# The 512 outputs of a decode step as eight rows of 64 on partitions 16 apart, by products in four column groups

## The chip, the cores and the metric

The kernel runs on one core of a Trainium2 chip. Its engines are TensorE (PE; its loading of weights is shown as PEld), VectorE (DVE), ScalarE (ACT), GpSimd (POOL) and SyncE (SP), which here only issues transfers; 16 DMA engines move the data. The metric is the device time of one execution in microseconds (us), the median of the runs. The kernel before takes 354.38 us (3 runs, 354.29 to 354.51).

## The reference, cut to what matters

One token of width 512 passes a block with modulated layer norms (shift, scale and gate from a vector c), an attention over a cache of 32768 positions with 32 query heads on 8 key/value heads, and a feed-forward part of 512 by 1792 by 512.

```python
mod = (_silu(c) @ w_mod).reshape(c.shape[0], 6, 1, -1)
sa, ca, ga, sb, cb, gb = (mod[:, 0].copy(), mod[:, 1].copy(), mod[:, 2].copy(), mod[:, 3].copy(), mod[:, 4].copy(), mod[:, 5].copy())
h = _layernorm(x, axis=-1) * (1 + ca) + sa
x = x + ga * _A_ref(h, A_k_cache, A_v_cache, A_wq, A_wo)
h = _layernorm(x, axis=-1) * (1 + cb) + sb
x = x + gb * _B_ref(h, B_w1, B_w2)
return x
```

`_A_ref` is the attention with its projections wq and wo, `_B_ref` is `relu(h @ w1) @ w2`. The change touches the last line of it: how `h @ w2`, the gate gb and the residual x are laid out when they meet.

## The kernel before, in words

All large tensors come by one queue, SP's, in an order written out by hand (`stream`): half of the first keys, w_mod, wq, then keys and values of the eight groups, then wo in four pieces, w1 in one, and w2 in five pieces (`W2P`: slices 0 to 4, 5 to 9, 10 and 11, 12, 13; a slice is 128 rows of w2, one row in each partition). They land in a ring of three slots; the last slot, `tail_sb`, holds wo, w1, w2 and some small work areas.

At the front, POOL and DVE make constants out of an identity matrix while the first transfers run: `cmask` (which group of 16, 8 or 4 partitions a partition belongs to), `place32` (a partition's number modulo 32, one column for each), and `rowpick`, of 34 columns, of which 30 to 33 hold a one where the partition belongs to that quarter of 32. The vectors c and x are brought into columns (L248, L254), the six modulation vectors are computed from w_mod (L324) and turned into columns `modT_sb`.

The middle is a loop over eight groups of heads. For each, DVE transposes the keys (L441), PE computes scores (L460), softmax runs on ACT and DVE, and PE multiplies with the values (L523). `build_qbd` (L415, on POOL) makes the weights of the scores for each group and reads the four ones of `rowpick` as a mask. PE's and DVE's order is written out by hand (`manual_schedule`).

The end: `project` multiplies with wo; x1T, the residual after attention, stands as 128 partitions by 4 columns. `layernorm_T` follows, and while its sums run (`meanwhile`), `expand` and `four_rows` turn x1T into four rows of 128 on partitions 30 to 33: DVE multiplies the columns with `place32` into 128 by 128 (L356), and one product with `rowpick` as weights sums them into the rows (L365). The gate `gb` takes the same way much earlier (L372). Then come 16 products with w1 (L765), a transpose and the relu (L775, L776) into `hid_st`, a strip of zeros with one hidden column every 32, and the products with w2 (L788): four for each slice, of 128 columns each. Output column block i belongs on partition 30 + i; the window of 32 (or 2) columns of `hid_st` that serves as weights is chosen so that the hidden column falls on that row, and the other rows get zeros. So blocks 0 and 1 go to the first column group of the array (partitions 0 to 31), and 2 and 3 to the second. At last DVE multiplies with the gate rows (L793), adds the residual rows (L795), and SP stores four rows of 256 bytes (L796). `keep_clock` issues products whose result is not used, between the steps of the tail.

Of the kernel before, what the change touches and what calls it, by code (L numbers as in the profile page):

```python
# [9 lines left out]
BF16 = mybir.dt.bfloat16  # L10
F32 = mybir.dt.float32
ACT = mybir.ActivationFunctionType
ALU = mybir.AluOpType
AX = mybir.AxisListType
# [3 lines left out]
def kernel(  # L18
# [14 lines left out]
    nc = tc.nc  # L33
    P = 128
    _, _, D = A_x.shape
# [3 lines left out]
    KT = D // P  # L39
    Dff = B_w1.shape[1]  # L40
    FT = Dff // P
# [10 lines left out]
    W2P = [(0, 5), (5, 10), (10, 12), (12, 13), (13, 14)]  # L52
    W1P = [(0, KT)]

    OUT0, OUT1 = 30, 34

    UNEVEN, EDGE, MOST = ("k", 0, (2, 3)), 2 * TK * Dh - D // 2, 111
    SPACE = 14
# [23 lines left out]
    const = ctx.enter_context(tc.tile_pool(name="const", bufs=1))  # L82
# [10 lines left out]
    loaded, last_loop, end_b = {}, [], []  # L93
# [3 lines left out]
    WO, TAIL = Hq * D, Hq * D + KT * Dff + FT * D  # L97

    def room(name, at, shape):

        n = 2
        for d in shape[1:]:
            n *= d
        return piece(name, at, n)[0:shape[0]].bitcast(F32)
# [77 lines left out]
    for i, row in enumerate((c[0], A_x[0, 0])):  # L182
# [4 lines left out]
    ident_f = const.tile([P, P], F32)  # L187
# [5 lines left out]
    R0 = WM + WQ  # L193
# [3 lines left out]
        out=sel.rearrange("p (h par) (a c) -> p h par a c", h=2, a=4),  # L197
        in_=AP(ib.tensor, ib.offset, [ib.ap[0], [64, 2], [1, 2], [0, 4], [2, 32]]),
    )
    QW = P + 4 * 7  # L200
    qbd = [const.tile([P, 4, QW], BF16, name=f"qbd{i}") for i in range(2)]
# [5 lines left out]
        out=mask16.rearrange("p (s q) -> p s q", q=REP),  # L207
        in_=AP(ident_f[:].tensor, ident_f[:].offset, [ident_f[:].ap[0], [0, 4], [1, REP], [REP, P // REP]]),
        op=ALU.add, axis=AX.X,
    )  # L210

    cmask, rsel = {}, {}
    for n in sorted({n * REP for _, n in WOP}):
# [20 lines left out]
    nc.vector.tensor_reduce(  # L234
        out=place32[:], in_=ident_f[:].rearrange("p (j m) -> p m j", m=32), op=ALU.add, axis=AX.X,
    )
    rowpick = const.tile([P, OUT1], F32)
    nc.gpsimd.memset(rowpick[:], 0.0)
    nc.vector.tensor_reduce(
        out=rowpick[:, OUT0:OUT1], in_=ident_f[:].rearrange("p (j m) -> p j m", m=32), op=ALU.add, axis=AX.X,  # L240
    )

    pick8 = const.tile([16, 8], BF16)
# [23 lines left out]
    def bank(name):  # L267
        return ps_s.tile([P, 512], F32, tag="m", name=name)[:]
# [85 lines left out]

    def expand(src_T, e):
        nc.vector.tensor_tensor(  # L356
            out=e, in0=src_T.unsqueeze(1).to_broadcast([P, 32, KT]),
            in1=place32[:].unsqueeze(2).to_broadcast([P, 32, KT]), op=ALU.mult,
        )
        return e  # L360

    def four_rows(e, name):

        r_ps = (end_b[0][:, 1, :] if end_b else bank(f"{name}_ps"))[0:OUT1, 0:P]
        nc.tensor.matmul(  # L365
            r_ps, lhsT=rowpick[:], rhs=e.rearrange("p m kt -> p (m kt)"), start=True, stop=True,
        )
        return r_ps

    gb_rows = const.tile([OUT1, P], F32)  # L370
    gb_exp = room("wmq_sb", R0 + 2048 + 8 * P, [P, 32, KT]).rearrange("p (m kt) -> p m kt", kt=KT)
    nc.scalar.copy(out=gb_rows[:], in_=four_rows(expand(modT_sb[:, 5 * KT:6 * KT], gb_exp), "gb"))  # L372

    hT = const.tile([P, KT], BF16)
    stat1 = const.tile([P, 2], F32)
# [35 lines left out]
    nc.vector.tensor_copy(out=qrep_sb[:], in_=qrep_ps[:])  # L411

    def build_qbd(g):
        d_ap, s_ap, m_ap = qbd[g % 2][:], qrep_sb[:], rowpick[:]
        nc.gpsimd.tensor_tensor(  # L415
            out=AP(d_ap.tensor, d_ap.offset + 4 * 7, [d_ap.ap[0], [QW, 4], [32, 4], [1, 4]]),
            in0=AP(s_ap.tensor, s_ap.offset + REP * g, [s_ap.ap[0], [Hq, 4], [0, 4], [1, 4]]),
            in1=AP(m_ap.tensor, m_ap.offset + OUT0, [m_ap.ap[0], [0, 4], [1, 4], [0, 4]]),
            op=ALU.mult,
        )  # L420

# [215 lines left out]
    with tc.manual_schedule(engines={mybir.EngineType.PE, mybir.EngineType.DVE}):  # L637
# [37 lines left out]
        g, h = LOOPED, LAST  # L675
# [69 lines left out]
        x1_ps = []  # L745

        def meanwhile():
            e = expand(x1T[:], room("tail_sb", TAIL + 1024, [P, 32, KT]).rearrange("p (m kt) -> p m kt", kt=KT))
            keep_clock(2)
            x1_ps.append(four_rows(e, "x1"))  # L750
            keep_clock(2)

        keep_clock(3)
        layernorm_T(x1T[:], stat2, h2T[:], modT_sb[:, 3 * KT:4 * KT], ncb[:], "ln2", meanwhile)
        x1_rows = const.tile([OUT1, P], F32)
        nc.vector.tensor_copy(out=x1_rows[:], in_=x1_ps[0])
        ffn_ps = end_b[0][0:OUT1, 1, P:2 * P]
        nc.vector.memset(ffn_ps, 0.0)

        NQ = 32 * FT  # L760
# [20 lines left out]
        for part, (f0, f1) in enumerate(W2P):  # L781
            w2_sb = need(("w2", part))
            for ft in range(f0, f1):
                for i in (0, 2, 1, 3):
                    row = OUT0 + i
                    to, w = (0, 32) if row < 32 else (32, OUT1 - 32)
                    at = 32 * ft + 31 - (row - to)
                    nc.tensor.matmul(  # L788
                        ffn_ps[to:to + w, :], lhsT=hid_st[:, at:at + w], rhs=w2_sb[:, ft - f0, i * P:(i + 1) * P],
                        start=False, stop=(ft == FT - 1 and i % 2 == 1), skip_group_check=True,  # L790
                    )
        o_rows = const.tile([OUT1, P], F32)
        nc.vector.tensor_tensor(out=o_rows[:], in0=ffn_ps, in1=gb_rows[:], op=ALU.mult)  # L793
        o_bf = const.tile([OUT1, P], BF16)
        nc.vector.tensor_tensor(out=o_bf[:], in0=o_rows[:], in1=x1_rows[:], op=ALU.add)  # L795
    nc.sync.dma_start(out=out[0, 0].rearrange("(i n) -> i n", i=KT), in_=o_bf[OUT0:OUT1])  # L796


# [28 lines left out]
```

## Time and profile before

The profile shows one execution, that of a run of 354.42 us.

| | before |
|---|---|
| median of 3 runs | 354.38 us |
| profiled execution, its run time | 354.42 us |
| profiled execution, its span | 352.6 us |
| PE busy | 272.3 us (77%), 1310 products |
| DVE busy | 195.6 us (55%), 167 instructions |
| ACT busy | 18.7 us (5%) |
| POOL busy | 6.0 us (2%) |
| read from HBM | 149.42 MB, 424 GB/s over the span |
| mean granted clock of PE | 0.926 of full speed |

A row of the profile gives the engine, the line of the kernel (L788), the operation, what it writes and reads, its shape (partitions x elements; for a product the array's rows * columns in use, then the moving data) and a count. Busy time is the time that an engine spends in instructions; products are pipelined, so the durations of single ones overlap, and a group's time is less than their sum. Idle time stands in brackets with what ended it. The span runs from the first to the last instruction, and the run time is some 1.8 us more.

### The profile page before, as it was taken

The numbers are of one execution on the slowest core, as the hardware profiler recorded it, in microseconds if no ns is written. First come the engines' busy times: TensorE is split into PE (matmuls) and PEld (weight loads), VectorE is DVE, ScalarE is ACT, GpSimd is POOL, SyncE is SP. The second block draws the span as 40 slices with busy tenths as digits, with TensorE's granted clock in tenths as the row PEclk, the third lists the DMA queues.
The fourth block names the chain that finished last, engine by engine and source line by source line (L and its number), as shares of the span: only waits on it lengthen the run. The fifth ranks groups of instructions, "written<-read, shape, count | busy, mean of one in ns | idle before, by whom it ended". The sixth has DMA issues, their size and how long they took to land. (4 is left out here: it accounts for less than half of the span.)

```text
span 352.6 us, 3544 instructions
## 1 busy us (share of the span) xinstructions
PE 272.3 (77%) x1310; PEld 111.8 (32%) x1310; DVE 195.6 (55%) x167; ACT 18.7 (5%) x37; POOL 6.0 (2%) x26
## 2 busy tenths in 40 slices
PE   0054980695999679884988499976999999789994
PEld 0021330232333224331333233322444443234442
DVE  7662563983079513965099316956674293743142
ACT  1200003001000010001000100001000100011000
POOL 3000000000000000000000000000000000000000
PEclk9996895698999969998999979996999999999999
DMA  8999989999999999999999999999999999999995
GB/s 353 404 432 456 468 387 461 446 401 446 439 424 440 416 439 446 401 455 446 409 453 446 409 453 431 426 394 439 446 414 427 450 429 424 431 453 398 432 426 213
DMA packets 5222, 149.57 MB, mean 424 GB/s; under 512 B 604, under 2 KB 988, under 8 KB 1628
## 3 DMA queue, kind: packets, MB, share of 16 engines
q1 hardware_dynamic: 5180, 149.43, 98.5%
q8 instruction: 8, 0.13, 0.1%
q14 instruction: 2, 0.02, 0.0%
q10 hardware_dynamic: 32, 0.00, 0.0%
HBM read 149.42 MB, written 0.00 MB: 424 GB/s over the span
## 5 line engine op out<-in xcount | busy, mean ns | idle before, releaser
L441 DVE STREAM_TRANSPOSE Ksb<-Ksb 128x4096 f32<-128x4096 f32 (+1 forms) x34 | 131.5, 3912 | 57.6 <-DMA Ksb<-in_A_k_cache_dram 57.6
L460 PE MATMUL S_ps<-Ksb,qbd 128*128 128x512 bf16 x512 | 118.9, 385 | 19.2 <-DVE Ksb L441 18.3
L523 PE MATMUL o_ps<-Vsb,P_g 128*16 (+1 forms) x512 | 124.3, 401 | 10.9 <-ACT P_g L497 10.0
L460 PEld LDWEIGHTS <-qbd 128*128 128x128 bf16 x512 | 49.2, 97 | 84.9 <-issue 27.6
L523 PEld LDWEIGHTS o_ps<-Vsb,P_g 128*16 x320 | 30.4, 95 | 60.0 <-issue 31.8
L523 PEld LDWEIGHTS <-P_g 128*16 128x16 bf16 x192 | 16.7, 90 | 22.9 <-issue 0.4
L473 DVE TENSOR_REDUCE m_p<-S_ps 128x1 f32<-128x1024 f32 x7 | 8.6, 1223 | 21.8 <-PE S_ps L460 21.8
L502 DVE STREAM_TRANSPOSE P_g<-P_g 128x1024 bf16<-128x1024 bf16 x8 | 10.0, 1245 | 15.6 <-ACT P_g L497 15.6
L494 ACT ACTIVATE nbias<-Mb_ps 128x1 f32<-128x1 f32 x8 | 1.4, 171 | 269.5 <-PE Mb_ps L492 269.5
L324 PE MATMUL mod_ps<-wmq_sb,siluT 128*1 128x512 bf16 x24 | 3.6, 624 | 9.9 <-DMA wmq_sb<-in_w_mod_dram 9.9
L332 DVE STREAM_TRANSPOSE Ksb<-Ksb 128x4096 f32<-128x4096 f32 x2 | 8.8, 4424 | 1.7 <-DMA Ksb<-in_A_k_cache_dram 1.7
L478 PE MATMUL mT_ps<-ident_f,m_p 128*1 128x128 f32 x8 | 2.2, 270 | 8.9 <-DVE m_p L473 7.9
L497 ACT ACTIVATE P_g<-S_ps,nbias 128x1024 bf16<-128x1024 f32 x8 | 8.9, 1114 | 0.2
L560 PE MATMUL acc_ps<-mask_sb,Y 16*128 16x4 f32 x16 | 3.4, 282 | 5.1 <-DVE Y L556 5.1
L552 DVE SCALAR_TENSOR_TENSOR o_ps<-o_ps,Linv,smask 16x512 f32<-16x512 f32 x8 | 5.8, 720 | 2.8 <-PE o_ps L523 2.8
L254 PE MATMUL xc_ps<-cx_sel,wmq_sb 16*128 16x2 bf16 x4 | 0.3, 172 | 8.7 <-DVE wmq_sb L248 8.7
L590 DVE CAST o_sb<-o_ps 128x4 bf16<-128x4 f32 (+2 forms) x4 | 0.7, 167 | 11.1 <-PE o_ps L586 11.1
L415 POOL TENSOR_TENSOR qbd<-qrep_sb,rowpick 128x64 bf16<-128x64 bf16 x8 | 2.4, 299 | 228.0 <-PE S_ps L460 198.3
L509 DVE RECIPROCAL Linv<-L_ps 16x1 f32<-16x1 f32 x8 | 1.0, 126 | 8.3 <-PE L_ps L506 8.3
L556 DVE TENSOR_REDUCE Y<-o_ps 16x128 f32<-16x512 f32 x8 | 5.4, 679 | 0.3
L635 PE MATMUL spare_ps<-qbd,ident_bf 128*128 128x512 bf16 x18 | 5.4, 381 | 0.0
L396 PE MATMUL q_ps<-wmq_sb,hT 128*1 128x512 bf16 x32 | 3.6, 626 | 2.3 <-DMA wmq_sb<-in_A_wq_dram 2.3
(114 smaller groups left out, 71.6 us busy)
## 6 DMA issues: line engine op xcount, KB each, us to landing
Ksb<-in_A_k_cache_dram SPq DMA_DIRECT2D x5, 4096.0 KB, 22.9
Vsb<-in_A_v_cache_dram SPq DMA_DIRECT2D x5, 4096.0 KB, 36.5
wmq_sb<-in_A_wq_dram SPq DMA_DIRECT2D x1, 4096.0 KB, 28.1
Vsb<-in_A_v_cache_dram SPq DMA_DIRECT2D x2, 2048.0 KB, 41.1
Ksb<-in_A_k_cache_dram SPq DMA_DIRECT2D x1, 4032.0 KB, 37.2
wmq_sb<-in_w_mod_dram SPq DMA_DIRECT2D x1, 3072.0 KB, 18.9
tail_sb<-in_A_wo_dram SPq DMA_DIRECT2D x1, 2048.0 KB, 23.2
tail_sb<-in_B_w_dram SPq DMA_DIRECT2D x1, 1792.0 KB, 30.6
```

The costliest lines, as they stand in the source:

```text
L324: nc.tensor.matmul(dst[j // 4][32 * (j % 4):32 * (j % 4) + 1, :], lhsT=src_T[:, kt:kt + 1], rhs=w[:, kt, j * 512:(j + 1) * 512], start=(kt ...
L332: nc.vector.transpose(out=t, in_=t)
L396: nc.tensor.matmul(q_ps[i][32 * a:32 * a + 1, :].rearrange("o (h e) -> o h e", e=32), lhsT=hT[:, kt:kt + 1], rhs=wq_f[:, kt, i, a], start= ...
L441: t = nc.vector.transpose(out=KTt.bitcast(F32), in_=KTt.bitcast(F32))
L460: nc.tensor.matmul(S_ps_tiles[g], lhsT=qbd[g % 2][:, hp, 4 * (7 - s):4 * (7 - s) + P], rhs=KTv[:, 16 * sl:16 * sl + 16, h, :, par], start= ...
L473: behind_loop(nc.vector.reduce_max(out=m_p[:], in_=S_g.rearrange("p g f -> p (g f)"), axis=AX.X))
L497: nc.scalar.activation(out=P_g[:], in_=S_g.rearrange("p g f -> p (g f)"), func=ACT.Exp, bias=nbias[:], scale=scale, accum_out=l_g[:],)
L502: behind_loop(nc.vector.transpose(out=P_g[:], in_=P_g[:]))
L523: nc.tensor.matmul(o_tiles[g][:], lhsT=PT, rhs=Vx, start=first, stop=False, skip_group_check=True)
L552: nc.vector.scalar_tensor_tensor(out=o, in0=o, scalar=Linv_tiles.pop(g)[:], in1=smask[:].unsqueeze(2).to_broadcast([16, 4, Dh]), op0=ALU.m ...
L556: nc.vector.tensor_reduce(out=Y[:], in_=o.rearrange("p s d -> p d s"), op=ALU.add, axis=AX.X)
L635: nc.tensor.matmul(spare[0], lhsT=ident_bf[:], rhs=qbd[0][:, :, 0:P], start=True, stop=True)
```

## The change

The outputs are laid out as eight rows of 64 on partitions 0, 16, 32 up to 112. For each slice of w2 there are eight products of 64 columns: for b = 0 and 1 and each of the four column groups a, block 2a + b goes to partition 32a + 16b; the weights are a window of 1 or of 17 columns of `hid_st`. The gate and the residual rows are made in the same layout: `expand` now multiplies with a new `place16` (128 by 64), and `eight_rows` takes a `rowpick` with a one in column 16i where the partition belongs to group i of 16, copied on POOL from `cmask[16]`. The mask that `build_qbd` read out of `rowpick` is a tensor of its own now (`quarter`). The last two operations of DVE run over 113 partitions of 64 elements, and the store takes eight rows of 128 bytes from partitions 16 apart.

```diff
@@ -52,7 +52,7 @@
     W2P = [(0, 5), (5, 10), (10, 12), (12, 13), (13, 14)]
     W1P = [(0, KT)]
 
-    OUT0, OUT1 = 30, 34
+    OUTP, ON = 113, D // 8
 
     UNEVEN, EDGE, MOST = ("k", 0, (2, 3)), 2 * TK * Dh - D // 2, 111
     SPACE = 14
@@ -234,10 +234,18 @@
     nc.vector.tensor_reduce(
         out=place32[:], in_=ident_f[:].rearrange("p (j m) -> p m j", m=32), op=ALU.add, axis=AX.X,
     )
-    rowpick = const.tile([P, OUT1], F32)
+    quarter = const.tile([P, 4], F32)
+    nc.vector.tensor_reduce(
+        out=quarter[:], in_=ident_f[:].rearrange("p (j m) -> p j m", m=32), op=ALU.add, axis=AX.X,
+    )
+    place16 = const.tile([P, 16], F32)
+    nc.vector.tensor_reduce(
+        out=place16[:], in_=ident_f[:].rearrange("p (j m) -> p m j", m=16), op=ALU.add, axis=AX.X,
+    )
+    rowpick = const.tile([P, P], F32)
     nc.gpsimd.memset(rowpick[:], 0.0)
-    nc.vector.tensor_reduce(
-        out=rowpick[:, OUT0:OUT1], in_=ident_f[:].rearrange("p (j m) -> p j m", m=32), op=ALU.add, axis=AX.X,
+    nc.gpsimd.tensor_copy(
+        out=rowpick[:].rearrange("p (i m) -> p i m", m=16)[:, :, 0], in_=cmask[16][:],
     )
 
     pick8 = const.tile([16, 8], BF16)
@@ -354,22 +362,22 @@
 
     def expand(src_T, e):
         nc.vector.tensor_tensor(
-            out=e, in0=src_T.unsqueeze(1).to_broadcast([P, 32, KT]),
-            in1=place32[:].unsqueeze(2).to_broadcast([P, 32, KT]), op=ALU.mult,
+            out=e, in0=src_T.unsqueeze(1).to_broadcast([P, 16, KT]),
+            in1=place16[:].unsqueeze(2).to_broadcast([P, 16, KT]), op=ALU.mult,
         )
         return e
 
-    def four_rows(e, name):
-
-        r_ps = (end_b[0][:, 1, :] if end_b else bank(f"{name}_ps"))[0:OUT1, 0:P]
+    def eight_rows(e, name):
+
+        r_ps = (end_b[0][:, 1, :] if end_b else bank(f"{name}_ps"))[0:OUTP, 0:ON]
         nc.tensor.matmul(
-            r_ps, lhsT=rowpick[:], rhs=e.rearrange("p m kt -> p (m kt)"), start=True, stop=True,
+            r_ps, lhsT=rowpick[:, 0:OUTP], rhs=e.rearrange("p m kt -> p (m kt)"), start=True, stop=True,
         )
         return r_ps
 
-    gb_rows = const.tile([OUT1, P], F32)
-    gb_exp = room("wmq_sb", R0 + 2048 + 8 * P, [P, 32, KT]).rearrange("p (m kt) -> p m kt", kt=KT)
-    nc.scalar.copy(out=gb_rows[:], in_=four_rows(expand(modT_sb[:, 5 * KT:6 * KT], gb_exp), "gb"))
+    gb_rows = const.tile([OUTP, ON], F32)
+    gb_exp = room("wmq_sb", R0 + 2048 + 8 * P, [P, 16, KT]).rearrange("p (m kt) -> p m kt", kt=KT)
+    nc.scalar.copy(out=gb_rows[:], in_=eight_rows(expand(modT_sb[:, 5 * KT:6 * KT], gb_exp), "gb"))
 
     hT = const.tile([P, KT], BF16)
     stat1 = const.tile([P, 2], F32)
@@ -411,11 +419,11 @@
     nc.vector.tensor_copy(out=qrep_sb[:], in_=qrep_ps[:])
 
     def build_qbd(g):
-        d_ap, s_ap, m_ap = qbd[g % 2][:], qrep_sb[:], rowpick[:]
+        d_ap, s_ap, m_ap = qbd[g % 2][:], qrep_sb[:], quarter[:]
         nc.gpsimd.tensor_tensor(
             out=AP(d_ap.tensor, d_ap.offset + 4 * 7, [d_ap.ap[0], [QW, 4], [32, 4], [1, 4]]),
             in0=AP(s_ap.tensor, s_ap.offset + REP * g, [s_ap.ap[0], [Hq, 4], [0, 4], [1, 4]]),
-            in1=AP(m_ap.tensor, m_ap.offset + OUT0, [m_ap.ap[0], [0, 4], [1, 4], [0, 4]]),
+            in1=AP(m_ap.tensor, m_ap.offset, [m_ap.ap[0], [0, 4], [1, 4], [0, 4]]),
             op=ALU.mult,
         )
 
@@ -745,16 +753,16 @@
         x1_ps = []
 
         def meanwhile():
-            e = expand(x1T[:], room("tail_sb", TAIL + 1024, [P, 32, KT]).rearrange("p (m kt) -> p m kt", kt=KT))
+            e = expand(x1T[:], room("tail_sb", TAIL + 1024, [P, 16, KT]).rearrange("p (m kt) -> p m kt", kt=KT))
             keep_clock(2)
-            x1_ps.append(four_rows(e, "x1"))
+            x1_ps.append(eight_rows(e, "x1"))
             keep_clock(2)
 
         keep_clock(3)
         layernorm_T(x1T[:], stat2, h2T[:], modT_sb[:, 3 * KT:4 * KT], ncb[:], "ln2", meanwhile)
-        x1_rows = const.tile([OUT1, P], F32)
+        x1_rows = const.tile([OUTP, ON], F32)
         nc.vector.tensor_copy(out=x1_rows[:], in_=x1_ps[0])
-        ffn_ps = end_b[0][0:OUT1, 1, P:2 * P]
+        ffn_ps = end_b[0][0:OUTP, 1, P:P + ON]
         nc.vector.memset(ffn_ps, 0.0)
 
         NQ = 32 * FT
@@ -781,19 +789,23 @@
         for part, (f0, f1) in enumerate(W2P):
             w2_sb = need(("w2", part))
             for ft in range(f0, f1):
-                for i in (0, 2, 1, 3):
-                    row = OUT0 + i
-                    to, w = (0, 32) if row < 32 else (32, OUT1 - 32)
-                    at = 32 * ft + 31 - (row - to)
-                    nc.tensor.matmul(
-                        ffn_ps[to:to + w, :], lhsT=hid_st[:, at:at + w], rhs=w2_sb[:, ft - f0, i * P:(i + 1) * P],
-                        start=False, stop=(ft == FT - 1 and i % 2 == 1), skip_group_check=True,
-                    )
-        o_rows = const.tile([OUT1, P], F32)
+                for b in range(2):
+                    at, w = 32 * ft + 31 - 16 * b, 1 + 16 * b
+                    for a in range(4):
+                        i = 2 * a + b
+                        nc.tensor.matmul(
+                            ffn_ps[32 * a:32 * a + w, :], lhsT=hid_st[:, at:at + w],
+                            rhs=w2_sb[:, ft - f0, i * ON:(i + 1) * ON],
+                            start=False, stop=(ft == FT - 1 and b == 1), skip_group_check=True,
+                        )
+        o_rows = const.tile([OUTP, ON], F32)
         nc.vector.tensor_tensor(out=o_rows[:], in0=ffn_ps, in1=gb_rows[:], op=ALU.mult)
-        o_bf = const.tile([OUT1, P], BF16)
-        nc.vector.tensor_tensor(out=o_bf[:], in0=o_rows[:], in1=x1_rows[:], op=ALU.add)
-    nc.sync.dma_start(out=out[0, 0].rearrange("(i n) -> i n", i=KT), in_=o_bf[OUT0:OUT1])
+        o_bf = const.tile([P, ON], BF16)
+        nc.vector.tensor_tensor(out=o_bf[0:OUTP], in0=o_rows[:], in1=x1_rows[:], op=ALU.add)
+    nc.sync.dma_start(
+        out=out[0, 0].rearrange("(i n) -> i n", n=ON),
+        in_=o_bf[:].rearrange("(i m) n -> i m n", m=16)[:, 0],
+    )
 
 
 # ---- launch: one core; inputs and outputs as the reference has them ----
```

## The prediction

> **What bounds the kernel now.** I read the page first, then the chain of waits, then the table of stretches, and last the timeline of the final ten microseconds.
>
> ```profile
> span 352.6 us, 3544 instructions
> DMA  8999989999999999999999999999999999999995
> q1 hardware_dynamic: 5180, 149.43, 98.5%
> q8 instruction: 8, 0.13, 0.1%
> ```
>
> One queue carries 149.43 MB and keeps the 16 DMA engines busy for 98.5% of the span; only the first and the last of the 40 slices fall below 9. The kernel is a stream of weights and cache, and work on the other engines costs time only where the stream is not running. The stretches say where that is (busy time of each engine, then the granted clock of PE, the DMA share, GB/s):
>
> ```profile
> 318.00:349.62 31.62, 29.53 (x242) 12.88 (x240) 8.37 (x29) 1.09 (x4) 0.00 (x0) 1.00 0.96 406
> 349.62:352.60 2.98, 0.28 (x4) 0.10 (x3) 0.57 (x2) 0.00 (x0) 0.00 (x0) 0.80 0.01 3
> ```
>
> The DMA share is 0.96 up to 349.62 us and 0.01 behind it. The last 3 us are a bare tail, and the chain of waits with the last issue of the timeline names its parts:
>
> ```profile
> 338.50 11.12 DMA tail_sb<-in_B_w_dram
> 349.66 0.29 PE end_ps L788 x4
> 349.98 0.29 DVE o_rows L793
> 350.30 0.28 DVE o_bf L795
> 350.61 0.29 SPq L796 DMA_DIRECT2D out_dram<-o_bf  x1
> ```
>
> The last piece of w2 (one of 14 slices) lands at 349.62. Four products (0.29), two operations on VectorE (0.29 and 0.28), and then the output's transfer and the close of the program, 352.6 − 350.61 = 2.0 us, follow one behind the other. The change works on these parts. Everything else that it touches lies ahead of 349.62 and must show up as a later landing or as a backlog on PE at that moment, or it costs nothing.
>
> **The products.** Each slice of w2 takes four products of 128 columns now, two in each of two column groups, and eight of 64 columns afterwards, two in each of four groups. The rows for the price:
>
> ```profile
> 347.10 0.73 PE L788 MATMUL end_ps<-tail_sb 128*32 128x128 bf16 x20
> 348.30 1.64 PE L788 MATMUL end_ps<-tail_sb 128*32 128x128 bf16 x36 [0.47 <-DMA tail_sb<-in_B_w_dram]
> 345.33 0.36 PE L765 MATMUL hid_ps<-tail_sb,h2T 128*1 128x448 bf16 x4 [1.28 <-DMA tail_sb<-in_B_w_dram]
> 345.33 0.93 PE L765 MATMUL hid_ps<-tail_sb,h2T 128*1 128x448 bf16 x16 [1.28 <-DMA tail_sb<-in_B_w_dram]
> 340.60 0.24 PE L622 MATMUL acc_ps<-tail_sb,place 128*32 128x4 f32 x8
> 341.01 0.67 PE L605 MATMUL acc_ps<-o_sb,tail_sb 128*128 128x1 bf16 x16
> L788 PE MATMUL end_ps<-tail_sb x56: 216/219/231, 347.1 to 349.7; 128*32 128x128 bf16 x28, 128*2 128x128 bf16 x28
> L765 PE MATMUL hid_ps<-tail_sb,h2T x16: 350/352/353, 345.3 to 345.9; 128*1 128x448 bf16 x16
> L622 PE MATMUL acc_ps<-tail_sb,place x8: 172/183/194, 340.6 to 340.7; 128*32 128x4 f32 x8
> L605 PE MATMUL acc_ps<-o_sb,tail_sb x32: 166/172/193, 339.7 to 341.5; 128*128 128x1 bf16 x32
> ```
>
> Twenty products of L788 take 0.73 us, one alone 0.219: 0.51 us for nine further pairs, 57 ns a pair. That is about the streaming of 128 columns, since one product's duration grows by (352 − 219) / (448 − 128) = 0.42 ns a column. Four groups do run side by side: four products of L765, 352 ns each, fill 0.36 us together, and sixteen (four rounds of four) fill 0.93, so a round comes every (0.93 − 0.352) / 3 = 193 ns, or 0.43 ns a column. A round of four products of 64 columns is then 28 ns if columns set it. If the loading of weights and the issue set it, the nearest row is L622, four groups with next to no columns: (0.24 − 0.183) / 7 = 8 ns a product, 33 ns a round. A slice of w2 thus costs two rounds, 56 to 66 ns, against two pairs, 114 ns now: PE gets faster, not slower, and no backlog grows.
>
> For the last piece the first product of the second round starts one round after the first and the last one some 25 ns later; a product of 64 columns lasts 219 − 64 × 0.42 = 192 ns. That is 0.03 + 0.02 + 0.19 = 0.24 us where four take 0.29: **−0.05** (bounds −0.06 and −0.03). The earlier slices keep their cover: they are done before 349.62 now at 114 ns each, and sooner afterwards.
>
> A rule of the Trainium skill speaks against this. TensorE: Matmul & The Clock Gate, section "Wait — 56ns, not 53.3ns?", has starts of successive matmuls never closer than about 25 ns, however few the columns; by it a slice would cost 200 ns, and the time would be 354.6 (worked out among the rivals). The row of four L765 products inside 0.36 us disagrees where they lie in different column groups: by the rule three gaps alone would add 0.075 us to the 0.352 of one.
>
> **The two operations on VectorE.** They go from 34 × 128 to 113 × 64.
>
> ```profile
> L740 DVE TENSOR_TENSOR x1T<-acc_ps,modT_sb x1: 164/164/164, 341.7 to 341.7; 128x4 f32<-128x4 f32 x1
> L356 DVE TENSOR_TENSOR tail_sb<-x1T,place x1: 284/284/284, 342.3 to 342.3; 128x128 f32<-128x128 f32 x1
> ```
>
> 128 partitions × 128 take 284 ns, as 34 × 128 do in L795, so partitions are free; 128 × 4 take 164. (284 − 164) / 124 = 0.97 ns an element, and 64 elements fewer save 62 ns, twice: **−0.12** (bounds −0.09 and −0.13).
>
> **The output's transfer.** Eight rows of 128 bytes leave from partitions 16 apart, where four of 256 bytes left from neighbours. No row shows such a store; the nearest are the two loads into eight partitions of 128 bytes each:
>
> ```profile
> L183 ACTq DMA_DIRECT2D cx_row<-in_c_dram x1: 588/588/588, 0.7 to 0.7; - x1
> L183 ACTq DMA_DIRECT2D cx_row<-in_A_x_dram x1: 282/282/282, 1.4 to 1.4; - x1
> ```
>
> Their issue takes 282 ns, or 588 for the first of the program, and L796 now takes 293. So the bounds are −0.01 and +0.30, and I take **0**, after the second one: L796 is the 38th issue of its queue, not the first. The bytes can't save anything (1 KB is nothing at 406 GB/s), and the 2.0 us stay.
>
> **What is moved ahead of the tail** costs nothing, by these covers:
>
> ```profile
> 5.80 0.35 DVE L234 TENSOR_REDUCE place<-ident_f 128x32 f32<-128x128 f32 x1
> 7.99 0.68 DVE L248 TENSOR_TENSOR wmq_sb<-cx_row,pick 16x512 bf16<-16x512 bf16 x1 [1.50 <-DMA cx_row<-in_A_x_dram]
> L223 POOL CAST rsel<-rsel_f x3: 188/191/198, 4.9 to 5.9; 128x4 bf16<-128x4 f32 x1, 128x8 bf16<-128x8 f32 x1, 128x16 bf16<-128x16 f32 x1
> L415 POOL TENSOR_TENSOR qbd<-qrep_sb,rowpick 128x64 bf16<-128x64 bf16 x8 | 2.4, 299 | 228.0 <-PE S_ps L460 198.3
> 345.30 0.50 PEld L765 LDWEIGHTS <-h2T 128*1 128x1 bf16 x16 [1.75 <-DVE end_ps L758]
> ```
>
> At the front VectorE makes one more reduction (place16, like L234, 0.35 us; quarter takes the place of L239). It lies ahead of L248, before which VectorE idles 1.50 us for the load of c and x. Without that cover 0.35 us would move to L248, and the mask products behind it have their own wait, 9.9 us, for w_mod. On POOL the memset grows and a copy of 0.19 us (as L223) is new; it waits for cmask[16], which VectorE makes before it, and behind it in the queue stands only L415, which idles 228 us in all. Near the end, expand and the copy of the x1 rows halve, the weights of the row product grow from 34 to 113 columns, and L758 shrinks. All of that precedes L765, which waits 1.28 us for w1 to land (rows above), so gain and loss both vanish there. Transfers of the stream and their order are the same.
>
> **The sum.** The profiled execution took 354.42 us, 1.8 more than its span of 352.6. −0.05 − 0.12 + 0 = −0.17 gives 354.25. The median of the runs shown, 354.38, lies 0.04 below the profiled one, so I predict **354.2**, −0.05%. What a measurement of this kernel can tell from no change is taken as 0.2%, or 0.7 us; the whole tail that the change can touch, leaving out the transfer, is 0.29 + 0.29 + 0.28 plus gaps, under 1 us. A gain past that bound would have to remove nearly all of it.
>
> **Rivals.**
>
> *Products that don't overlap (slower).* If each of the eight products pays its own gap instead of sharing a round, PE becomes the bound between 348.30, when the second piece of w2 has landed, and the end: nine slices are left, 72 products. At today's mean gap of (0.73 − 0.219) / 19 = 27 ns the last starts at 348.30 + 71 × 0.027 = 350.22 and ends at 350.41, 0.46 later than now; less VectorE's 0.12, the time is 354.7. At the gap of L605, whose weights fill the whole array, (0.67 − 0.172) / 15 = 33 ns, it ends at 350.85: 355.2, slower by 0.2%. It costs from some 21 ns a product, where 72 of them outlast the landing of the last piece. L765 and L622 speak against it (8 ns a product); for it only that neither has narrow weights and 64 columns at once. Chance 7%. At the 25 ns of the page named above, the end would be 350.27, and the time 354.6.
>
> *Code on a DMA engine.* PE gets 112 more instructions. The page's second queue brings instructions, 8 packets in 0.13 MB, 16 KB each, whose time is 0.1% of 16 engines' span: 0.001 × 16 × 352.6 / 8 = 0.7 us a packet (0.35 to 1.06, by the rounding). A ninth packet on the engine that finishes the stream last would delay the landing by that: 354.9, up to 355.3. The trace doesn't tell where a packet ends in the program. Chance 6%.
>
> *The clock falls.* Stretches of 3.41 us, cut where the granted clock changes (columns as above: PE's busy time comes first, the granted clock stands third from the right):
>
> ```profile
> 156.83:160.25 3.42, 2.10 (x11) 0.76 (x9) 1.32 (x2) 0.00 (x0) 0.30 (x1) 1.00 1.10 479
> 160.25:163.66 3.41, 0.83 (x4) 0.47 (x4) 1.65 (x4) 1.35 (x3) 0.00 (x0) 1.00 0.93 404
> 201.21:204.62 3.41, 1.80 (x5) 0.72 (x6) 1.73 (x2) 1.06 (x2) 0.00 (x0) 0.50 0.89 384
> 204.62:208.03 3.41, 3.41 (x10) 1.10 (x8) 0.00 (x0) 0.00 (x0) 0.00 (x0) 0.50 0.89 384
> 344.57:347.98 3.41, 2.42 (x39) 1.14 (x40) 0.71 (x2) 0.47 (x2) 0.00 (x0) 1.00 1.00 401
> ```
>
> With 2.10 us of PE work the next stretch kept 1.00, with 1.80 it had 0.50. The stretch ahead of the last products has 2.42; the five slices of L788 in it, ten rounds of 28 ns and the end of the last product, take 0.45 instead of 0.73, which leaves 2.14, just above. If the clock falls, a round takes 56 ns and a product some 30 ns more, 0.06 us in all: 354.3. Chance 10%.
>
> *A dearer store*, at its upper bound of +0.30: 354.5. Chance 8%.
>
> **How the numbers follow.** The forecast has 59% (354.0 to 354.4), the falling clock 10%, the store 8%, the non-overlap 7%, the code 6%; 10% are left for what no row shows, half on either side. Faster by over 0.7 us is only in that rest and some of the forecast's own scatter: 7%. Slower by over 0.7 us takes half of the non-overlap, a third of the code and the other half of the rest: 11%. The range holds the forecast, the clock, the store and the low ends of non-overlap and code: 353.9 to 354.8.
>
> **What would show it.** In the profile after: the landing of the last piece still about 349.6; L788's line with 112 products whose last eight end within 0.25 us; two operations on VectorE of 222 ns; an issue of about 0.29 us, and 2.0 us from it to the end. A landing later by 0.4 us or more, a ninth packet of instructions, or products that still run when the last piece lands would make the prediction wrong.

## The result and the profile after

The changed kernel takes 355.92 us (median of 9 runs, 355.08 to 356.74) where the kernel before takes 354.36 (9 runs beside them). The ratio is 1.0047, with an interval of 1.0039 to 1.0055: slower by half a per cent, outside the predicted range, and on the other side of the predicted 354.2. Single executions, of the kernel before too (one of 370.82 us among the 9), take over 2% longer than the rest; the ratios and intervals leave them out, and so does the median of 355.51 us below.

The profiled execution of the changed kernel took 355.92 us. Its page, in the rows that were read first before:

```profile
span 353.5 us, 3658 instructions
...
DMA  8999989999999999999999999999999999999994
...
q1 hardware_dynamic: 5188, 149.43, 98.2%
q8 instruction: 8, 0.13, 0.1%
```

The stream is what it was: the same 149.43 MB, the DMA engines as busy, the same count of packets on q8, a queue that brings instructions. There are 114 instructions more, and only the last slice of the DMA line is lower. So the loss lies in the tail again. The chain of waits (start, length in us, what) shows it:

```profile
331.00 17.80 DMA tail_sb<-in_B_w_dram
348.80 0.04 issue
348.85 0.25 PE end_ps L796 x9
349.09 0.79 issue
349.88 0.51 PE end_ps L796 x23
...
350.41 0.24 DVE o_rows L802
...
350.67 0.23 DVE o_bf L804
```

Before, the chain went from the landing of the last piece of w2 to four products. Now it leaves the third piece (slices 10 and 11), runs nine products, and then TensorE stands still for 0.79 us with "issue" as the reason: it waited for nothing that the profile shows. The last 23 products follow. The stretches around that pause (busy time of PE, PEld, DVE, ACT, POOL, then the granted clock, the DMA share and GB/s):

```profile
348.25:349.09 0.84, 0.71 (x49) 0.47 (x49) 0.00 (x0) 0.00 (x0) 0.00 (x0) 1.00 0.36 123
349.09:349.88 0.79, 0.00 (x1) 0.00 (x0) 0.00 (x0) 0.00 (x0) 0.00 (x0) 1.00 0.01 3
349.88:350.39 0.51, 0.49 (x23) 0.31 (x22) 0.00 (x0) 0.00 (x0) 0.00 (x0) 0.50 0.00 0
```

In the pause TensorE doesn't compute and doesn't load weights, nor does any other engine work, and the stream is over (DMA share 0.01). What was waiting had its data: 23 products run off in one go behind it. The clock of the 23 products is 0.50, but the fall comes with the pause's end and not before; they take 0.51 us. The timeline has the products that ran without a pause, the end of the tail, and the store's issue:

```profile
346.96 0.47 PE L796 MATMUL end_ps<-tail_sb 128*1 128x64 bf16 x40
...
350.41 0.23 DVE L802 TENSOR_TENSOR o_rows<-end_ps,gb_rows 113x64 f32<-113x64 f32 x1 [3.52 <-PE end_ps L796]
350.67 0.23 DVE L804 TENSOR_TENSOR o_bf<-o_rows,x_rows 113x64 bf16<-113x64 f32 x1
350.93 0.69 SPq L805 DMA_DIRECT2D out_dram<-o_bf  x1
```

Forty products, five slices, take 0.47 us, where twenty took 0.73. The two operations of VectorE take 0.23 us each, where they took 0.29 and 0.28. The issue of the store takes 0.69 us, where it took 0.29. Put side by side, the two profiled executions (354.42 and 355.92 us) differ like this:

| part | before | after | difference |
|---|---|---|---|
| end of the last product | 349.95 | 350.39 | +0.44 |
| from there to the store's issue | 0.66 | 0.54 | −0.12 |
| from the issue to the end of the span | 1.99 | 2.57 | +0.58 |
| run time outside the span | 1.82 | 2.42 | +0.60 |
| sum | 354.42 | 355.92 | +1.50 |

VectorE's part came as predicted. Three costs are new, each some half a microsecond: a pause of TensorE, a slower store, and time outside the span that no engine's row shows. The experiments take them one by one.

### The profile page after: what moved, and what is told of

The parts are those of the page before. It is cut to its first block, busy times and chain, and to the rows that moved or that the text cites. A ratio compares the mean times of both kernels' runs of the same rounds, so it can differ in the third digit from the quotient of the medians.

```text
span 353.5 us, 3658 instructions
## 1 busy us (share of the span) xinstructions
PE 273.2 (77%) x1366; PEld 112.2 (32%) x1366; DVE 195.7 (55%) x168; ACT 18.6 (5%) x37; POOL 6.2 (2%) x27
## 3 DMA queue, kind: packets, MB, share of 16 engines
q1 hardware_dynamic: 5188, 149.43, 98.2%
## 5 line engine op out<-in xcount | busy, mean ns | idle before, releaser
L468 PE MATMUL S_ps<-Ksb,qbd 128*128 128x512 bf16 x512 | 120.7, 391 | 17.8 <-DVE Ksb L449 17.0
L423 POOL TENSOR_TENSOR qbd<-qrep_sb,quarter 128x64 bf16<-128x64 bf16 x8 | 2.3, 293 | 228.1 <-PE S_ps L468 198.3
L489 DVE TENSOR_REDUCE Mrow<-mT_ps 1x4 f32<-1x128 f32 x8 | 2.2, 274 | 5.6 <-PE mT_ps L486 5.6
```

The source lines that it names most:

```text
L468: nc.tensor.matmul(S_ps_tiles[g], lhsT=qbd[g % 2][:, hp, 4 * (7 - s):4 * (7 - s) + P], rhs=KTv[:, 16 * sl:16 * sl + 16, h, :, par], start= ...
```

## Experiments on the pause

Two theories stood at first. One: TensorE's program has grown at its end by 56 products with as many loads of weights, and the pause is a wait for instructions that the instruction queue brings. The DMA view of the 1 us from 347.4 on (packets, MB, share of 16 engines) shows the last packet of 0.02 MB (16 KB: 8 packets are 0.13 MB):

```profile
q1 hardware_dynamic: 210, 0.27, 72.1%
q8 instruction: 1, 0.02, 5.8%
```

The other: the new order of products (four column groups, 64 columns) stalls the array at some point, whatever the code. If it is code, the length of TensorE's program ahead of the tail must matter. The middle of the kernel has a loop whose body holds 16 products in one round of the hand-written order and 4 in the rest; this number can be changed without a change in what is computed, and all code behind it moves.

**A shorter program, after.**

```diff
-        nb = 4 if g == HALVED - 1 else 1
+        nb = 1
```

> The changed kernel, with the one loop over products of the values that is written out four times (L525) written out once, so that PE has some 120 instructions fewer in its program and runs the same ones. In the changed kernel's profile PE stands still for 0.79 us at 349.1, inside the third piece of w2, for nothing that the profile shows, and ends at 350.39 instead of 349.95; the run lasts 2.42 us longer than the span instead of 1.78. Theory (PE's program has grown past a limit of what has been brought by then): the pause is gone, PE ends at about 349.9, and the part outside the span goes back to 1.8: 354.8. Rival (the pause comes from the products themselves, their weights or their column groups): pause and time stay, 355.9. Half-way (the pause is the code, the part outside the span isn't): 355.4.

Measured: 355.51 us, ratio 1.0037 [1.0024, 1.0050]: neither the theory's 354.8 nor the rival's 355.9, but near the half-way 355.4. But the pause isn't gone, which the half-way case takes for granted; the profiled execution has a smaller and later one:

```profile
349.37 0.20 PE end_ps L796 x3
349.56 0.37 issue
349.93 0.24 PE end_ps L796 x5
```

It starts behind the third of the last eight products, the 107th of 112, where it started behind the 89th before. So the pause moved when only the code's length was changed, which the theory of a stall in the array doesn't explain. (The clock was 0.50 here from about 345.2 to 348.65 us, 1.00 in the changed kernel, so the two tails differ in that as well.) And it moved by 18 products only, fewer than the edit removes from the program with its 12 products in one loop body and their address instructions; how far the pause moves isn't explained by length alone.

**The same edit, before.**

> The kernel before with the same loop written out once, as a control: what the loop itself is worth. Theory of the code: the kernel before has no pause, so nothing changes, 354.4. Rival (the shorter loop costs or saves something by itself, which would also stand in the first run): up to 0.5 us either way.

Measured: 354.31 us, 1.0001 [0.9992, 1.0009]. The loop's body in itself costs and gains nothing.

**A longer program, before.** Two rounds now have 16 products in the body.

```diff
-        nb = 4 if g == HALVED - 1 else 1
+        nb = 4 if g >= HALVED - 2 else 1
```

> The kernel before with a second loop over products of the values written out four times: some 120 instructions more in PE's program, as many as the change adds (112), at an earlier place; the products run are the same. If only the length of the program counts: PE pauses among the products with w2, ends about 0.7 us later, and the part outside the span grows by 0.6: 355.6. If it counts where in the program a packet of instructions is asked for and when it lands: the packet is asked for earlier in time here, there is no pause, and only the part outside the span grows, 355.0. If code has nothing to do with it: 354.4.

Measured: 354.21 us, 1.0001 [0.9992, 1.0010], and no pause. So a longer program alone doesn't cost anything, and the part outside the span doesn't grow with it, though two of the three expected cases had that.

**A longer program, after**, with the same edit.

> The changed kernel with a second loop over products of the values written out four times, as in the third run: PE's program grows by another 120 instructions at an earlier place. Theory (what counts is when the last packet of PE's instructions lands, and it is asked for some 120 instructions ahead of its place in time): the packet lands at about 343 instead of 347.4, the pause of 0.79 us is gone although the program is longer than ever, PE ends at 349.9, 355.2, and the runs lie close together instead of over 1.7 us. Rival (the length of the program counts): a pause at least as long as in the changed kernel, 355.9 or more.

Measured: 355.15 us (355.08 to 355.35), 1.0028 [1.0017, 1.0038]. The pause is gone. The chain of waits has the form that was predicted, from the landing of the last piece at 349.35 on:

```profile
338.22 11.13 DMA tail_sb<-in_B_w_dram
349.35 0.04 issue
349.39 0.26 PE end_ps L796 x8
...
349.67 0.24 DVE o_rows L802
...
349.93 0.22 DVE o_bf L804
```

A longer program is faster here by 0.77 us (355.92 − 355.15), which only a dependence on where the code lies can bring, and the same products in the same order run without a stall. The pause is not all of this gain. In the means of the runs it is 0.73 us, of which 0.41 lie in the span (353.22 against 352.81), where the pause is, and 0.32 outside it; the next section comes back to those. The packets of q8 fit a wait for code, without proving it: in this kernel the packet that stood at 347.4 comes at 343.1 (DMA view of the 1 us from there), with the stream still at its full share, and a ninth follows from 349.1 on, as the stream ends:

```profile
q1 hardware_dynamic: 51, 0.40, 95.8%
q8 instruction: 1, 0.02, 5.8%
...
q8 instruction: 1, 0.02, 8.8%
```

That a packet as late as 347 is harmless while less code lies behind it is shown by the kernel before itself, which has one in the 1 us from 347.7 on, and no pause:

```profile
q1 hardware_dynamic: 207, 0.26, 69.6%
q8 instruction: 1, 0.02, 5.8%
```

The same program has it at 344.2 in three other profiled executions (those of the experiments below that change only VectorE, POOL or the store of the kernel before), so the time at which a packet moves scatters by 3.5 us with TensorE's program unchanged. With the 56 products of the kernel before behind it, that scatter did no harm. With 112 the packet's time alone doesn't explain the pause: in the four profiled executions that have one, here and below, the packet moves between 347.25 and 347.75 us, while the pause begins at 348.83 to 349.56 and lasts 0.37 to 1.07 us. The runs of the changed kernel have spans from 352.7 to 353.7 us, and the shortest, a run of 355.08 us, has a span as short as without the pause.

The Trainium skill, Runtime: NRT & Kernel Launch, section "Instruction fetch mechanics", states that an engine's instructions are refilled in blocks of 16 KiB over a DMA queue of its own, and that crossing such a block is mostly hidden. The trace agrees on the size of q8's packets (8 in 0.13 MB). That the pause is such a crossing isn't shown; if it is, it was not hidden, but cost 0.37 to 1.07 us of standing still.

## Experiments on the time outside the span

The kernel with the longer program still has 355.30 − 352.8 = 2.5 us outside the span where the kernel before has 1.8. The DMA view covers the time behind the span as well. Before, from 352.6 on, and after, from 353.5 on:

```profile
DMA packets 0, 0.00 MB, mean 0 GB/s; under 512 B 0, under 2 KB 0, under 8 KB 0
```
```profile
DMA packets 1, 0.01 MB, mean 1 GB/s; under 512 B 0, under 2 KB 0, under 8 KB 0
...
q14 instruction: 1, 0.01, 0.5%
```

One packet of instructions, on another queue (q14) and of 0.01 MB, moves behind the end of the changed kernel, at about 355.6 us, and none behind the one before (within the span each of the two has two of q14). q14 isn't TensorE's queue of the packets above, so the suspects are the engines whose programs have grown: POOL (a copy) and VectorE (one reduction).

**POOL's program shorter, after**, by the memset of a tensor that nothing reads.

```diff
-    ones_f = const.tile([P, P], F32)
-    nc.gpsimd.memset(ones_f[:], 1.0)
```

> The changed kernel without one memset on POOL, of a tensor that nothing reads, so that POOL has as many instructions as in the kernel before. In the changed kernel, the first run and the fourth, the run lasts 2.3 to 2.4 us longer than its span, against 1.8 in the kernel before and the third run, whatever the length of PE's program and the store. Theory P (POOL's program has grown by one instruction over a limit): 1.8 us outside the span, time lower by 0.6, 355.3. Theory V (VectorE's has): nothing changes, 355.9.

Measured: three runs of 355.05 to 355.25 and three of 356.85 to 356.97, 1.0045 [1.0026, 1.0064]. The packet of q14 is still there, so POOL isn't its cause. The profiled execution is one of the longer ones, and its view behind the span (from 353.3 on) shows why they are longer:

```profile
q8 instruction: 1, 0.02, 2.2%
q14 instruction: 1, 0.01, 0.6%
```

A ninth packet of q8 moves there as well, and 356.97 − 353.3 = 3.7 us lie outside the span. Three of the nine runs of the changed kernel have 3.2 to 3.3 us there, and five of the twelve of the kernel with the store from neighbours (below) 3.1 to 3.6, which fits the same packet, though no profile of one of those was taken. With the longer TensorE program, whose ninth packet moves within the span, no run has it: the runs have 2.1 to 2.5 us outside. So the longer program took away two things, the pause and this.

**VectorE's program longer, before**, by the one reduction that the change adds, its result unused.

```diff
+    place16 = const.tile([P, 16], F32)
+    nc.vector.tensor_reduce(
+        out=place16[:], in_=ident_f[:].rearrange("p (j m) -> p m j", m=16), op=ALU.add, axis=AX.X,
+    )
```

> The kernel before with one reduction more on VectorE at the front (place16, which nothing reads), so that VectorE has as many instructions as in the changed kernel. Theory V: 2.4 us outside the span instead of 1.8, time 354.8. Theory P: nothing changes, 354.2.

Measured: 354.64 us against 354.26, 1.0009 [1.0000, 1.0018]. Its profiled execution has 354.73 − 352.5 = 2.2 us outside the span, and the packet behind it:

```profile
q14 instruction: 1, 0.01, 0.4%
```

In all 12 runs 2.05 to 2.48 us lie outside the span, in the runs of the kernel before beside them 1.75 to 1.85.

**VectorE's program shorter, after.** On top of the longer TensorE program, a reduction that makes a 16 by 4 mask gives way to a part of `cmask` that holds the same numbers.

```diff
-    smask = const.tile([16, 4], F32)
-    nc.vector.tensor_reduce(
-        out=smask[:], in_=ident_f[0:16, 0:16].rearrange("p (s q) -> p s q", q=REP), op=ALU.add, axis=AX.X,
-    )
+    smask = cmask[REP][0:16, 0:4]
```

> The changed kernel with the two loops written out four times (no pause of PE, 355.15 in the fifth run) and with one reduction less on VectorE (the mask smask is read out of cmask[4], which holds the same ones), so that VectorE has as many instructions as in the kernel before. Theory (one instruction more on VectorE than the kernel before costs 0.4 to 0.6 us outside the span): outside it 1.8 us, time 354.7. Rival (that part comes with the longer program of PE): 2.4 us and 355.15 as in the fifth run.

Measured: 354.63 us (354.49 to 354.81), 1.0014 [1.0005, 1.0023], 0.52 less than with the instruction. Outside the span lie 354.63 − 352.9 = 1.7 us, 1.73 to 1.89 in all 11 runs, and no packet moves there.

**VectorE's program shorter, before**, by the same edit.

> The kernel before with one reduction less on VectorE (smask read out of cmask[4]). If VectorE's program has passed a limit in the changed kernel: nothing changes on this side of it, 354.25, 1.8 us outside the span. If every instruction on VectorE costs by itself: 353.85.

Measured: 354.15 us, 0.9999 [0.9990, 1.0008]. One instruction fewer gains nothing here, one more costs 0.4: a limit lies between 167 and 168 instructions of VectorE, not a price for each. All six kernels whose page counts 168 instructions of VectorE have the packet behind the span, and the eight with 167 or fewer have none. One run contradicts this: among the 11 of the kernel without all three costs (below, 167 instructions) one, of 355.02 us, has 2.42 us outside its span; it has no profile.

## Experiments on the store

**Eight neighbouring rows, after.** The number and size of the rows stay.

```diff
-        in_=o_bf[:].rearrange("(i m) n -> i m n", m=16)[:, 0],
+        in_=o_bf[0:8],
```

> The changed kernel with the store taking partitions 0 to 7 instead of 0, 16, up to 112 (so seven of the eight rows that it writes are not the result). In the changed kernel the store's issue takes 0.69 us (0.29 before) and 2.58 us pass from it to the end of the span (2.04 before). Theory (the step of 16 partitions costs it): issue 0.29, 2.04 us, time 355.4. Rival (eight rows in place of four cost it): issue 0.69, time 355.9.

The issue falls from 688 to 318 ns (rows of the changed kernel and of this one, by line):

```profile
L805 SPq DMA_DIRECT2D out_dram<-o_bf x1: 688/688/688, 350.9 to 350.9; - x1
```
```profile
L805 SPq DMA_DIRECT2D out_dram<-o_bf x1: 318/318/318, 350.8 to 350.8; - x1
```

and from the issue to the end of the span it is 352.9 − 350.8 = 2.1 us instead of 2.57 (before: 1.99 by the table above). The median of the runs, 355.47 (1.0034 [1.0022, 1.0047]), says little of it, since the pause is still there and scatters: five of twelve runs lie at 354.45 to 354.85, the others at 355.24 to 356.53, and the profiled one, at 355.24, has a pause of 1.07 us:

```profile
348.58 0.25 PE end_ps L796 x9
348.83 1.07 issue
349.91 0.39 PE end_ps L796 x23
```

It lies behind the 89th product, as in the changed kernel, though it starts 0.26 us earlier; the kernel with POOL's shorter program has it there too, from 349.27 on. TensorE's program is the same in the three, so the pause keeps its place in the program and not in time. The 23 products take 0.39 us here, at a clock of 1.00.

**Four rows 32 apart, before.** `o_bf` becomes 128 partitions, zeroed at the front in place of the unread tensor, and the store reads partitions 0, 32, 64 and 96.

```diff
-    nc.sync.dma_start(out=out[0, 0].rearrange("(i n) -> i n", i=KT), in_=o_bf[OUT0:OUT1])
+    nc.sync.dma_start(
+        out=out[0, 0].rearrange("(i n) -> i n", i=KT),
+        in_=o_bf[:].rearrange("(i m) n -> i m n", m=32)[:, 0],
+    )
```

> The kernel before with its store taking four rows from partitions 0, 32, 64 and 96 instead of 30 to 33 (so three of its four rows are zeros; the memset that makes them takes the place of another on POOL). Theory (a step between the partitions makes the store's issue long, whatever the number of rows): issue about 0.7 us instead of 0.29, time 354.7. Rival (only eight rows with a step): issue 0.3, time 354.2.

Measured: 354.76 us against 354.26, 1.0015 [1.0006, 1.0024].

```profile
L795 SPq DMA_DIRECT2D out_dram<-o_bf x1: 627/627/627, 350.6 to 350.6; - x1
```

Four rows, as before, and the issue takes 627 ns: the step between the partitions is dear, not the number of rows. Both dear stores also spread over the whole 128 partitions, and both cheap ones lie close together; a step within a few neighbouring partitions wasn't tried.

**All three costs taken away, after.** The longer program of TensorE, VectorE's shorter one and the store from neighbouring partitions stand together, by the edits shown above.

> As the run before, and with the store taking partitions 0 to 7 instead of eight rows 16 apart (so seven of the rows that it writes are not the result): the products and the two operations on VectorE of the change, without its three costs (pause, store, VectorE's one instruction). If these three are all, the prediction's sum is left: -0.15 against the kernel before, 354.1. If something is left that isn't found, 354.3 or more.

Measured: 354.11 us, 0.9999 [0.9990, 1.0007], 0.52 less than without the last step. The tail in the chain of waits, and the store's issue in the timeline:

```profile
349.34 0.26 PE end_ps L793 x8
...
349.62 0.23 DVE o_rows L799
...
349.88 0.22 DVE o_bf L801
```
```profile
350.13 0.32 SPq L802 DMA_DIRECT2D out_dram<-o_bf  x1
```

So the three costs account for the loss, within the 0.3 us that the interval leaves either way. Step by step, in medians: 355.92, with the longer TensorE program (no pause, no ninth packet of q8 behind the span) 355.15, without the instruction of VectorE 354.63, with a store from neighbours 354.11; the kernel before has 354.19 beside the last two.

## A version without the three costs

A kernel that computes the reference's outputs and avoids all three: the eight rows of 64 stand on neighbouring partitions, 28 to 35, so that four fall into the first column group and four into the second, and the products go in turn to the two.

```diff
-    OUT0, OUT1 = 30, 34
+    OUT0, OUT1, ON = 28, 36, D // 8
...
-                for i in (0, 2, 1, 3):
+                for i in (0, 4, 1, 5, 2, 6, 3, 7):
```

The mask `quarter` is made on POOL, by adding pairs of columns of `rowpick`; the memset that nothing reads is left out, and the longer loop and VectorE's shorter program are taken over.

> A version that should lose none of the three: eight rows of 64 on the neighbouring partitions 28 to 35, by eight products of 64 columns a slice in two column groups, the two loops written out four times, as many instructions on VectorE as before. The operations on VectorE at the end save 0.12, the last eight products, four rounds in two groups, end some 0.02 later than four do now: 354.15. If the longer program of PE or the smaller rows cost more than is seen so far: 354.3 or more.

Measured: 354.24 us, 1.0005 [0.9996, 1.0014], the kernel before 354.19. Its chain has the shorter operations on VectorE, but eight products in two groups behind the landing:

```profile
349.50 0.30 PE end_ps L790 x8
...
349.82 0.23 DVE o_rows L795
...
350.07 0.22 DVE o_bf L797
```

From the landing to the end of VectorE the tail is some 0.1 us shorter than before, which the runs can't tell from nothing. No version tried beats the kernel before.

## Why the prediction was wrong, by its steps

**The bound** was right: a stream up to 349.6 us, and behind it a bare tail in which each part counts in full. So was the small size of the gain: without the three costs the kernel takes 354.11 where the one before takes 354.19. (Of the DMA line the sixth slice too lies below 9, not only the first and the last; that changes nothing in the argument.)

**The products** were right in mechanism and size. Ten rounds of four take (0.47 − 0.193) / 9 = 31 ns each, where 28 to 33 were expected (0.193 us is the duration of one product of 64 columns; 0.192 were expected). The last eight take 0.26 us where 0.24 were expected and four took 0.29: −0.03 instead of −0.05, at the edge of the bounds. The rival of products that don't overlap falls by the same row, and so does the rule of 25 ns between starts that the Trainium skill gives in TensorE: Matmul & The Clock Gate, section "Wait — 56ns, not 53.3ns?": by it forty products would take 39 × 0.025 + 0.19 = 1.17 us, where the trace has 0.47.

**VectorE's operations** were right: 225 ns each, 222 expected, and −0.12.

**The output's transfer** failed: "Their issue takes 282 ns, or 588 for the first of the program, and L796 now takes 293. So the bounds are −0.01 and +0.30, and I take **0**". It is +0.5: the issue grew by 0.40 (688 against 293 ns), and the rest follows behind it. The rows chosen as nearest were loads whose partitions are neighbours, as those of the store before are; the step of 16 partitions, the one thing that was new, had no row, and the bounds were drawn as though it had. A bound from rows that lack the property in question is no bound. The rival of a dearer store had the right place, with a price too small and 8%.

**The code** failed in its way and its weight. The rival took a ninth packet to be a later landing of the stream by 0.7 us, at 6%. The stream landed at its time (349.35 without the pause, where 349.62 was before); it was TensorE that waited, for a pause of 0.37 to 1.07 us in the profiled executions that have one. In the means of the runs the longer program, which moves the code, takes away 0.41 us in the span and 0.32 outside it. The number of packets didn't even rise in the profile that shows the pause. The prediction had counted the "112 instructions", but asked only on which DMA engine their packet would run, not whether TensorE might stand still among them in the one stretch where a wait counts in full.

**What is moved ahead of the tail** failed: it "costs nothing, by these covers". The covers were right for time: the reduction does lie in VectorE's wait at the front. What it costs lies behind the end: with one more instruction in VectorE's program a packet of q14 moves after the span, and 0.4 to 0.5 us go there. No part of the sum and no rival looked outside the span.

**The falling clock** came about in the profiled execution (0.50 from 349.88 on), and there it made the 23 products take 0.51 us instead of 0.39, so 0.12 us of its loss. It isn't the cause of the pause: in the kernel with the store from neighbours and in that with POOL's shorter program the clock stays at 1.00 over the 23 products behind the pause, and without the pause it is 1.00 to the end of the products. The 2.14 us of PE work that the prediction left in the stretch ahead of the last products was too much: without the pause the stretch from 346.82 to 350.23 has 1.87, and the clock falls at its end, too late to matter.

Summed up, the terms that were worked out from rows of the same kind held within 0.03 us; the three that were taken at nothing, or nearly so, made 1.8 us together in the medians (355.92 against 354.11).

**What stays open.** In the four profiled executions with a pause TensorE resumed at 349.75 to 349.93, more than 2.1 us after the last packet of q8 had moved, and the pause itself began over 1.0 us after it; so that TensorE waited for instructions is inferred from the edits to its program, and what filled that time isn't shown. Where in a program a packet begins isn't shown either, and that a q8 packet holds TensorE's instructions, and the one of q14 VectorE's, is inferred from the edits that move them. Why the shorter program moved the pause by 18 products only, and what the ninth packet of q8 behind the span holds, were not tried.

## What to carry to other kernels

Count a change's instructions for each engine and ask where the new code runs: at the very end of this kernel, behind the stream, nothing hid a pause among the new products, and even an instruction that is hidden in time at the front can lengthen what happens behind the last one. Then move the code on purpose, as the longer loop did here, and see whether the time changes. When a layout changes, look at the partitions of the transfer at its end first, since a step between rows can cost more than all that the layout gains on the engines (0.5 us here, against 0.1 to 0.2). And when a gain of 0.2 us is worked out from rows, the term at zero that has no row of its own kind deserves the wider bounds.

## What the runs showed of the hardware that was not expected

- A store of a few rows from partitions with a step between them is dear: 688 ns (eight rows, 16 apart) and 627 ns (four rows, 32 apart) for the issue, against 318 and 293 ns for eight and four neighbouring rows, and 0.5 us on the time in both kernels.
- One more instruction of VectorE, hidden in time, costs 0.4 to 0.5 us outside the span once a limit is crossed: 168 instead of 167 instructions bring a packet of 0.01 MB that moves some 2 us after the span's end.
- TensorE stood still for 0.37 to 1.07 us among its last products in four profiled executions, at one place in the program (behind the 89th of 112 products in the three with the same TensorE program); code added in an earlier loop took this away.
- A packet of the instruction queue q8 moved at 347.7 us in one profiled execution and at 344.2 in three others with the same TensorE program, while the stream was still running.
- Products in four column groups with one or 17 columns of weights start about 8 ns apart (31 ns for four), far closer than their own duration of 193 ns.
